# Second products of a two-matmul FFN issued in column halves of 256, and the last row's output evicted in quarters

## The chip, the cores and the metric

The kernel runs on one core of one Trainium2 chip. The metric is the device time of one execution in microseconds; the median of three runs is compared. TensorE multiplies, ScalarE (ACT), VectorE (DVE) and GpSimd (POOL) work elementwise, SyncE (SP) issues the DMAs.

## The reference

Windowed attention followed by a feed-forward network. Four batches, 8 heads, 768 positions, head size 64. Each position attends to its neighbours closer than 16 and to 24 block summaries (the maximum of 32 keys, the mean of 32 values). The heads of a position are joined to a row of 512, and the rows go through the network:

```python
x = attn_out.transpose(0, 2, 1, 3).reshape(B * S, H * D)      # 3072 x 512
h = x @ w_in                                                   # 512 -> 2048
r = np.maximum(h, 0.0)
g = s * (r * r) + b
out = g @ w_out                                                # 2048 -> 512
```

All is float32. The kernel reaches the accuracy by splitting each float32 operand into an upper part of the type fp32r and a lower part of the same type (what the upper leaves over), and adding three products: upper by lower, lower by upper, upper by upper.

## The kernel before

The 3072 rows are cut into 12 chunk rows ("c") of 256 rows. The hidden size 2048 is cut into 16 steps ("f") of 128. For each (c, f) there are:

- `hidden` (L444): the first products. Twelve matmuls of 256 columns into the PSUM tile `ph`: three terms by four slices of the 512 inputs. Stationary are slices of `wl_in` or `wh` (the lower and upper parts of w_in), moving are `xh` or `xl`.
- `activate`, `scaled`, `split_rows`: ScalarE's Relu (L452) and Square (L458), GpSimd's scale and offset (L466), VectorE's split into `gh` (L471) and `gl` (L473).
- `project` (L488): the second products. The 256 rows are two row halves t = 0, 1 of 128; each has a PSUM tile `po[t]` of 128x512, one bank, in which all 16 steps of a chunk row add up. Per t there are three matmuls of 512 columns: stationary is a 128x128 slice of `gl` or `gh`, moving is `w_h["out", f]` or `w_l["out", f]` ("wh" and "wl_out" in the profile; the upper parts of w_in and w_out of a step share a tile called wh).
- `evict` (L498 issues its DMA): after step 15 ScalarE copies `po[t]` to SBUF (the copy's line is L230, a helper; VectorE's copies are L228), and SP sends 256 KB to the output.

In chunk row 0 eight of the steps use plain float32 with one matmul instead of three; the other 184 (c, f) have three terms. The attention of the next chunk row is woven in between: transposes of the probabilities (pt, L358), products with the values (pav, L394), scores (ps, L308).

The order of the work is written out by the program, not found by a scheduler. A table gives the order for the first two chunk rows and the start of the third; after that every piece is put into `plan` at a step number i = 16 c + f with a rank within the step, and each engine's queue has its instructions in the order in which the pieces were called. The hidden products of four steps stand together (`i - i % 4`), and the second products of those four steps come together one group later (`(i + 4) | 3`). So TensorE's queue runs: 48 matmuls of hidden products, perhaps a piece of attention, 24 matmuls of second products, and again. After the last chunk row's hidden products two groups of second products follow each other, 48 matmuls, and then the two evictions.

Of the kernel before, what the change touches and what calls it, by code (L numbers as in the profile page):

```python
# [11 lines left out]
F32 = mybir.dt.float32  # L12
# [7 lines left out]
P = 128  # L20
B, H, S, D = 4, 8, 768, 64
DM, DFF = 512, 2048
# [7 lines left out]
T = NSUB * SUB  # L30
NPAIR = H // 2
PER_B = S // T
NC = B * PER_B
NST = S // SUB
NKC = DM // P
NF = DFF // P
# [8 lines left out]
def windowed_attention_then_relu2_ffn(ctx, tc, qk, vwin, kt, vt, kq, vrow, wp, out):  # L45


    nc = tc.nc
# [4 lines left out]
    stage = ctx.enter_context(tc.tile_pool(name="stage", bufs=4))  # L53
# [37 lines left out]
    def at(step, order, fn, *args):  # L91
        plan[step].append((order, len(plan[step]), fn, args))
# [5 lines left out]
    for base, sign in ((0, 1), (BLOCK - 1, -1)):  # L98
        nc.gpsimd.affine_select(
            out=mean4[:, NB - 4 : NB], in_=mean4[:, NB - 4 : NB], compare_op=ALU.is_ge, fill=0.0,  # L100
# [8 lines left out]
    def steps(c):  # L109
        return SECOND if c == 1 else tuple(range(NF))  # L110
# [32 lines left out]
    def whole(key):  # L143
        uses[key] += 1
        return w_f[key] if uses[key] < (2 if key[1] in THREE else 3) else w_f.pop(key)
# [80 lines left out]
    def copy(by_dve, out_, in_):  # L226
        if by_dve:
            nc.vector.tensor_copy(out_, in_)  # L228
        else:
            nc.scalar.copy(out_, in_)  # L230
# [7 lines left out]
    def place(c):  # L238
        return c // PER_B, c % PER_B
# [182 lines left out]
    ph_of, ph_both, r_of, gg, po = {}, {}, {}, {}, {}  # L422
# [50 lines left out]
        nc.vector.tensor_tensor(gl, g, gh.bitcast(F32), ALU.subtract)  # L473
        gg[c, f] = gh, gl

    def project(c, f):
        if f == steps(c)[0]:
            for t in range(T // P):
                po[t] = ps_po.tile([P, DM], F32, name="po", tag="po")
        g = gg.pop((c, f))  # L480
        if c == 0 and f not in THREE:
            terms = [(g[0], whole(("out", f)))]
        else:
            gh, gl = g
            terms = [(gl, w_h["out", f]), (gh, w_l["out", f]), (gh, w_h["out", f])]
        for t in range(T // P):
            for n, (a, w) in enumerate(terms):
                nc.tensor.matmul(  # L488
                    po[t], a[:, t * P : (t + 1) * P], w,
                    start=(f == steps(c)[0] and n == 0), stop=(f == steps(c)[-1] and n == len(terms) - 1),  # L490
                )

    def evict(c, t, other=False):
        o = stage.tile([P, DM], F32, name="o", tag="stage")
        copy(other, o, po[t])
        bi, ci = place(c)
        r0 = bi * S + ci * T + t * P
        nc.sync.dma_start(out[r0 : r0 + P, :], o)  # L498


    LOAD, SPLIT, ATT, NEXT, WEIGHTS, HID, PE_ATT, CHAIN, VISIT, PROJ, EVICT = range(11)
# [34 lines left out]
    def of(fn, s):  # L536
# [8 lines left out]
        "Ai": of(scale_weights, "in"), "Ao": of(scale_weights, "out"), "Bi": of(convert_weights, "in"),  # L545
        "Bo": of(convert_weights, "out"), "D": lambda f: convert_weights(("in", f), ("out", f)),
        "Y": hidden_part, "H": hidden, "J": activate, "G": scaled, "g": split_rows, "P": project, "O": evict,
        "hi": of(upper_weights, "in"), "ho": of(upper_weights, "out"), "li": of(lower_weights, "in"),
        "lo": of(lower_weights, "out"),
# [18 lines left out]
    def then(step, order, fn, *args):  # L568
        if (fn, args) not in ahead:
            at(step, order, fn, *args)  # L570

    for c in range(2, NC):
        bi, ci = place(c)
        for p in range(NPAIR):
# [3 lines left out]
            m, e0, e1, n, fv, tr, tu, va, xa = (base + lag for lag in lags)  # L578
# [27 lines left out]
    for i in range(NF, NC * NF):  # L606
        c, j = divmod(i, NF)
        f = steps(c)[j]

        then(i - i % 4, HID, hidden, c, f)  # L610
        for stage_of in (activate, scaled, split_rows):
            then(i, CHAIN, stage_of, c, f)
        then((i + 4) | 3, PROJ, project, c, f)
        if j == NF - 1:
            for t in range(T // P):
                then((i + 4) | 3, EVICT, evict, c, t)
# [60 lines left out]
```

## Time and profile before

| what | value |
|---|---|
| median of the runs | 630.85 us (630.57 to 630.95, 3 runs) |
| profiled execution | 630.93 us, its span 629.2 us |
| TensorE matmuls busy | 616.5 us, 5330 matmuls and as many weight loads |
| VectorE, ScalarE, GpSimd busy | 328.3, 308.7, 187.7 us |
| second products with three terms (L488) | 3 x 368 matmuls of 512 columns, mean 392 to 397 ns from start to end |
| hidden products with three terms (L444) | 3 x 704 matmuls of 256 columns, mean 276 to 278 ns |

Matmuls overlap: one starts long before the one ahead of it has ended. The mean duration is therefore not the pace; the pace is the distance between starts, which the chain of waits (length of a block over its number of matmuls) and the timeline show. "PEld" is the weight load that stands before each matmul.

### The profile page before, as it was taken

The page shows a single profiled execution, that of the slowest core. Times are in us where ns is not written, and L with a number is a line of the kernel's source. Part 1 is how long each engine was busy: PE and PEld are TensorE (multiplying, and loading weights), DVE is VectorE, ACT ScalarE, POOL GpSimd, SP SyncE. Part 2 cuts the span into 40 slices and gives each one's busy share as a digit, 9 for nine tenths or more (in the row PEclk, how much of TensorE's full clock was granted, in tenths as well). Part 3 has the DMA queues.
Part 4 walks back from the last instruction along what each step waited for, and adds up shares of the span by engine and source line. Part 5 has one row for each costly group of instructions (what it writes and reads, how often), then busy time and mean ns, then how long its engine had stood idle before and what let it go on. Part 6 is the DMA issues. An engine that isn't in the chain of part 4 may idle for free.

```text
span 629.2 us, 14328 instructions
## 1 busy us (share of the span) xinstructions
PE 616.5 (98%) x5330; PEld 550.7 (88%) x5330; DVE 328.3 (52%) x1092; ACT 308.7 (49%) x939; POOL 187.7 (30%) x351
## 2 busy tenths in 40 slices
PE   6999999999999999999999999999999999999997
PEld 5757878989989998999899999998998999899896
DVE  6999899865354246345454335336435324523311
ACT  4999975453463364265245426436345336323321
POOL 3126442211511422322242331341151151232211
PEclk9999999999999999999999999999999999999999
DMA  8999503006205015203502211600710500200000
GB/s 333 413 416 416 222 26 126 17 2 190 79 18 181 1 44 200 74 19 102 165 20 87 94 44 38 236 19 1 218 62 7 181 0 19 85 2 1 34 1 33
DMA packets 26997, 66.45 MB, mean 106 GB/s; under 512 B 3824, under 2 KB 3824, under 8 KB 26928
## 3 DMA queue, kind: packets, MB, share of 16 engines
q1 hardware_dynamic: 26928, 65.54, 29.3%
q8 instruction: 42, 0.69, 0.5%
q14 instruction: 27, 0.22, 0.1%
HBM read 59.09 MB, written 6.29 MB: 104 GB/s over the span
## 4 chain that ended last, share of the span: by engine, by line
PE 87%; DVE 4%; ACT 2%; issue 1%; POOL 1%; DVEq 0%; POOLq 0%; ACTq 0%
PE po L488 40%; PE ph L444 38%; PE pav L394 3%; PE pt L358 3%; PE ps L308 3%; DVE wf_out L141 1%; POOL g L466 1%; DVE wl_in L155 1%; DVE wf_in L141 0%; DVE wf_in L139 0%; ACT r L458 0%; DVE wf_out L139 0%; ACT wraw L125 0%; ACT wraw L126 0%; ACT r L452 0%
## 5 line engine op out<-in xcount | busy, mean ns | idle before, releaser
L466 POOL TENSOR_SCALAR g<-r,sb_col 128x256 f32<-128x256 f32 x189 | 127.1, 673 | 379.2 <-ACT r L458 256.0
L471 DVE CAST gh<-g 128x256 fp32r<-128x256 f32 x184 | 54.9, 298 | 244.0 <-POOL g L466 244.0
L452 ACT ACTIVATE r<-ph 128x256 f32<-128x256 f32 x179 | 67.6, 378 | 206.1 <-PE ph L444 187.0
L488 PE MATMUL po<-wh,gl 128*128 128x512 f32 x368 | 146.3, 397 | 0.0
L488 PE MATMUL po<-wh,gh 128*128 128x512 f32 x368 | 145.0, 394 | 0.0
L488 PE MATMUL po<-wl_out,gh 128*128 128x512 f32 x368 | 144.2, 392 | 0.0
L444 PE MATMUL ph<-xh,wl_in 128*128 128x256 f32 x704 | 109.9, 278 | 0.1
L444 PE MATMUL ph<-xl,wh 128*128 128x256 f32 x704 | 108.8, 276 | 0.0
L444 PE MATMUL ph<-xh,wh 128*128 128x256 f32 x704 | 108.7, 276 | 0.0
L473 DVE TENSOR_TENSOR gl<-g,gh 128x256 fp32r<-128x256 f32 x184 | 85.8, 466 | 33.6 <-PE po L488 16.4
L444 PEld LDWEIGHTS ph<-xh,wl_in 128*128 128x128 f32 x704 | 96.8, 188 | 4.8 <-issue 0.5
L444 PEld LDWEIGHTS ph<-xl,wh 128*128 128x128 f32 x704 | 93.6, 188 | 0.0
L444 PEld LDWEIGHTS ph<-xh,wh 128*128 128x128 f32 x704 | 93.0, 188 | 0.0
L339 ACT ACTIVATE pr<-pr,mn 128x120 f32<-128x120 f32 x176 | 67.0, 382 | 38.6 <-DVE mn L326 38.4
L458 ACT ACTIVATE r<-r 128x256 f32<-128x256 f32 x184 | 77.0, 418 | 15.2 <-DVE r L454 9.7
L488 PEld LDWEIGHTS po<-wh,gl 128*128 128x128 f32 x368 | 69.1, 188 | 14.8 <-issue 1.4
L488 PEld LDWEIGHTS po<-wh,gh 128*128 128x128 f32 x368 | 69.2, 188 | 14.3
L488 PEld LDWEIGHTS po<-wl_out,gh 128*128 128x128 f32 x368 | 69.2, 188 | 13.8
L270 POOL COPY vw<-vsum 24x256 f32<-24x256 f32 x88 | 41.7, 503 | 20.9 <-DMA vsum<-vmean 9.5
L230 ACT COPY o<-po 128x512 f32<-128x512 f32 x24 | 14.0, 589 | 42.3 <-PE po L488 41.3
L339 ACT ACTIVATION_READ_ACCUMULATOR pr<-pr,mn 128x1 f32 x176 | 33.0, 187 | 0.0
L349 DVE TENSOR_TENSOR pr<-pr,rs 128x480 f32<-128x480 f32 x48 | 32.0, 666 | 1.7
(90 smaller groups left out, 565.4 us busy)
## 6 DMA issues: line engine op xcount, KB each, us to landing
wraw<-in_wp_dram SPq DMA_DIRECT2D x32, 512.0 KB
qk<-in_qk_dram SPq DMA_DIRECT2D x44, 369.0 KB
vw<-in_vwin_dram SPq DMA_DIRECT2D x48, 256.0 KB
out_dram<-o SPq DMA_DIRECT2D x24, 256.0 KB
kraw<-in_kt_dram SPq DMA_DIRECT2D x12, 384.0 KB
vraw<-in_vt_dram SPq DMA_DIRECT2D x12, 252.0 KB
kq<-in_kq_dram SPq DMA_DIRECT2D x4, 512.0 KB
vraw<-in_vt_dram SPq DMA_DIRECT2D x6, 264.0 KB
```

Of the source, the lines that this page charges most:

```text
L270: nc.gpsimd.tensor_copy(vw_t[c, p][WIN:KR, e], vsum[bi][WIN : WIN + NB, 2 * p + e, :].unsqueeze(1).to_broadcast([NB, NSUB, D]),)
L308: nc.tensor.matmul(o, qi, kw[r, i, :], start=True, stop=True)
L339: nc.scalar.activation(pr, pr, AF.Exp, bias=mn_of[c, p][:, n : n + 1], scale=-1.0, accum_out=sm_of[c, p][:, n : n + 1])
L349: nc.vector.tensor_tensor(pr, pr, rs.unsqueeze(2).to_broadcast([P, 4, KR]), ALU.mult)
L358: nc.tensor.transpose(pt_of[c, p][:KR, n * P : (n + 1) * P], pr[:, n, :], ident)
L444: nc.tensor.matmul(ph, w[:, kc * P : (kc + 1) * P], x[:, kc], start=(n == 0), stop=(n == len(terms) - 1))
L452: nc.scalar.activation(r, ph, AF.Relu)
L458: nc.scalar.activation(r, r, AF.Square)
L466: (nc.vector if other else nc.gpsimd).tensor_scalar(g, r_of.pop((c, f)), s_col, b_col, ALU.mult, ALU.add)
L471: nc.vector.tensor_copy(gh, g)
L473: nc.vector.tensor_tensor(gl, g, gh.bitcast(F32), ALU.subtract)
L488: nc.tensor.matmul(po[t], a[:, t * P : (t + 1) * P], w, start=(f == steps(c)[0] and n == 0), stop=(f == steps(c)[-1] and n == len(terms) - 1),
```

## The change

Two parts. First, every three-term second product is issued in two halves of 256 columns: for each row half the three terms go to columns 0 to 255 and then to columns 256 to 511. The one-term products of chunk row 0 stay at 512 columns. Only the first matmul of a bank carries the start flag.

Second, in the last chunk row the last four steps are no longer taken step by step with both row halves each: all four steps are done for row half 0, then for row half 1. A new `evict_last` takes the place of the two evictions there: each 128x512 row half goes out as two tiles of 128x256, the left one copied by ScalarE, the right one by VectorE, with a DMA of 128 KB each.

```diff
-    def project(c, f):
+    def project(c, f, only=None):
...
-        g = gg.pop((c, f))
+        g = gg[c, f] if only == 0 else gg.pop((c, f))
...
-        for t in range(T // P):
-            for n, (a, w) in enumerate(terms):
-                nc.tensor.matmul(
-                    po[t], a[:, t * P : (t + 1) * P], w,
-                    start=(f == steps(c)[0] and n == 0), stop=(f == steps(c)[-1] and n == len(terms) - 1),
-                )
+        size = DM // 2 if len(terms) > 1 else DM
+        for t in range(T // P) if only is None else (only,):
+            for d in range(0, DM, size):
+                for n, (a, w) in enumerate(terms):
+                    nc.tensor.matmul(
+                        po[t][:, d : d + size], a[:, t * P : (t + 1) * P], w[:, d : d + size],
+                        start=(f == steps(c)[0] and n == 0 and d == 0),
+                        stop=(f == steps(c)[-1] and n == len(terms) - 1 and d == DM - size),
+                    )
...
+    def evict_last():
+        half = DM // 2
+        for t in range(T // P):
+            bi, ci = place(NC - 1)
+            r0 = bi * S + ci * T + t * P
+            for d in range(2):
+                o = stage.tile([P, half], F32, name="o", tag="stage")
+                copy(d == 1, o, po[t][:, d * half : (d + 1) * half])
+                nc.sync.dma_start(out[r0 : r0 + P, d * half : (d + 1) * half], o)
...
+        if c == NC - 1 and j >= NF - 4:
+            for t in range(T // P):
+                then((i + 4) | 3, PROJ + t, project, c, f, t)
+            if j == NF - 1:
+                then((i + 4) | 3, EVICT + 1, evict_last)
+            continue
```

TensorE's queue at one step of the second products, before: two row halves, three matmuls each (the number in a name tells tiles apart).

```order
L488 MATMUL po<-wh_745,gl 128x512
L488 MATMUL po<-wl_out_1040,gh 128x512
L488 MATMUL po<-wh_745,gh 128x512
L488 MATMUL po<-wh_745,gl 128x512
L488 MATMUL po<-wl_out_1040,gh 128x512
L488 MATMUL po<-wh_745,gh 128x512
```

The same step after the change:

```order
L490 MATMUL po<-wh_745,gl 128x256
L490 MATMUL po<-wl_out_1040,gh 128x256
L490 MATMUL po<-wh_745,gh 128x256
L490 MATMUL po<-wh_745,gl 128x256
L490 MATMUL po<-wl_out_1040,gh 128x256
L490 MATMUL po<-wh_745,gh 128x256
L490 MATMUL po<-wh_745,gl 128x256
L490 MATMUL po<-wl_out_1040,gh 128x256
L490 MATMUL po<-wh_745,gh 128x256
L490 MATMUL po<-wh_745,gl 128x256
L490 MATMUL po<-wl_out_1040,gh 128x256
L490 MATMUL po<-wh_745,gh 128x256
```

Twelve matmuls of half the width stand where six stood, each with its weight load; nothing moved in or out between them.

The end of ScalarE's queue and of SP's, before:

```order
L452 ACTIVATE r<-ph 128x256
L458 ACTIVATE r<-r 128x256
L230 COPY o<-po 128x512 x2
```

```order
L259 DMA vw<-in_vwin_dram 128x512 x3
L498 DMA out_dram<-o 128x512 x4
```

The ends of ScalarE's, VectorE's and SP's queues after it:

```order
L452 ACTIVATE r<-ph 128x256
L458 ACTIVATE r<-r 128x256
L230 COPY o<-po 128x256 x2
```

```order
L471 CAST gh<-g 128x256
L473 TENSOR_TENSOR gl<-g,gh 128x256
L228 COPY o<-po 128x256 x2
```

```order
L259 DMA vw<-in_vwin_dram 128x512 x3
L501 DMA out_dram<-o 128x512 x2
L511 DMA out_dram<-o 128x256 x4
```

ScalarE's two copies are halved, VectorE has two more at its end, and SP's last two DMAs became four of half the size. VectorE's copy of a bank waits for ScalarE's copy of the same bank in the compiled program.

## The prediction

> **What bounds the kernel now.** I read the page first, then the busy time by stretches, then the chain in order of time, and last single matmuls in the timeline. From the page, the span, TensorE's two rows (matmuls and weight loads) and the chain:
>
> ```profile
> span 629.2 us, 14328 instructions
> PE 616.5 (98%) x5330; PEld 550.7 (88%) x5330; DVE 328.3 (52%) x1092; ACT 308.7 (49%) x939; POOL 187.7 (30%) x351
> PEclk9999999999999999999999999999999999999999
> ...
> PE po L488 40%; PE ph L444 38%; PE pav L394 3%; PE pt L358 3%; PE ps L308 3%; DVE wf_out L141 1%; POOL g L466 1%; DVE wl_in L155 1%; DVE wf_in L141 0%; DVE wf_in L139 0%; ACT r L458 0%; DVE wf_out L139 0%; ACT wraw L125 0%; ACT wraw L126 0%; ACT r L452 0%
> ```
>
> The second products (po, L488) and the first ones (ph, L444) hold 78% of the chain. By stretches (length, then busy time of PE, PEld, DVE, ACT, POOL):
>
> ```profile
> 60.00:112.00 52.00, 50.24 (x381) 44.07 (x374) 47.73 (x132) 37.71 (x99) 19.19 (x27) 1.00 0.38 136
> 112.00:160.00 48.00, 48.00 (x423) 43.79 (x422) 34.17 (x105) 21.95 (x70) 11.93 (x19) 1.00 0.30 90
> 160.00:400.00 240.00, 240.00 (x2100) 218.82 (x2099) 106.56 (x399) 109.59 (x359) 72.38 (x138) 1.00 0.25 82
> 400.00:600.00 200.00, 200.00 (x1685) 182.45 (x1684) 81.21 (x279) 81.82 (x256) 57.06 (x108) 1.00 0.17 56
> ```
>
> From 112 us on TensorE never waits, at full clock, and no other engine is near its limit. What counts is the pace of its matmuls. The chain gives it by blocks, here the first TensorE block on it, one chunk row, and the end:
>
> ```profile
> 81.88 3.11 PE ph L444 x24
> ...
> 224.91 5.70 PE po L488 x24
> 230.61 5.47 PE ph L444 x48
> 236.08 5.49 PE po L488 x24
> 241.57 5.47 PE ph L444 x48
> 247.04 0.87 PE pt L358 x8
> 247.91 5.51 PE po L488 x24
> 253.43 5.46 PE ph L444 x48
> 258.89 0.87 PE pt L358 x8
> ```
>
> A block of 24 matmuls of 512 columns takes as long as one of 48 of 256. Both load a new 128x128 weight for every matmul, so the hidden stage is already the shape that the change gives the second products. The timeline resolves the pace (start, duration; a row of x4 is four matmuls):
>
> ```profile
> 609.00 0.64 PE L444 MATMUL ph<-xh,wl_in 128*128 128x256 f32 x4
> ...
> 610.39 0.62 PE L444 MATMUL ph<-xh,wl_in 128*128 128x256 f32 x4
> ...
> 614.47 0.39 PE L488 MATMUL po<-wh,gl 128*128 128x512 f32 x1
> ...
> 625.23 0.40 PE L488 MATMUL po<-wh,gh 128*128 128x512 f32 x1
> ```
>
> From 614.47 to 625.23 lie 47 steps of 512 columns: 10.76 / 47 = 228.9 ns each. From 610.39 to 614.47 lie 36 steps of 256: 4.08 / 36 = 113.3 ns. The first 12 of that block took 1.39 us, 115.8 ns each: a block that follows 512-column matmuls needs some steps to reach its pace, and that costs 1.39 - 12 x 0.1133 = 0.03 us.
>
> **The change, part by part.**
>
> 1. *Halves.* 1104 three-term matmuls (three groups of 368) become 2208 of 256 columns with 2208 weight loads. 24 of the 1104 lie before 81.88 us, where the chain is on other engines; 1080 count. Two halves at the settled pace are 226.7 ns against 228.9, a gain of 2.2 to 2.3 ns each: -2.4 us. I take the settled pace of the hidden stage because the instruction pair has the same form: an fp32r weight load of 128 columns, then 256 columns streamed. The other end is below under the rivals.
>
> 2. *Block starts.* 39 blocks of hidden products that now follow 512-column products will follow 256-column ones and need no settling: -39 x 0.03 = -1.2 us. 30 blocks of second products that start after transposes (pt) or after the value and score products (pav, ps) may have to settle themselves: +30 x 0.03 = +0.9 us. The 88 to 110 ns that such a block loses now (5.70 or 5.51 against 5.49 us) is its first weight load, which nothing covers; it stays. Net -0.3 us, between -1.2 and +0.9.
>
> 3. *More instructions.* 2208 more on TensorE's queue. The hidden stage issues at the same rate now without a gap, so this is put at nothing; cover gone, it would show as the settling cost above on every pair.
>
> 4. *Last four steps by row half.* The same 48 matmuls (96 halves) in another order. Step 12's operands come first in both orders; the last step's gl is needed about 9 x 0.23 = 2 us after the first of these products instead of 18 x 0.23 = 4 us. VectorE's last gl ends here, against products that start at 614.47 + 24 x 0.229 = 620.0 us, so nothing waits:
>
> ```profile
> 617.62 0.43 DVE L473 TENSOR_TENSOR gl<-g,gh 128x256 fp32r<-128x256 f32 x1
> ```
>
> 5. *The end.* Now:
>
> ```profile
> 624.97 1.28 ACT L230 COPY o<-po 128x512 f32<-128x512 f32 x2 [8.69 <-PE po L488]
> ...
> 625.58 1.02 SPq L498 DMA_DIRECT2D out_dram<-o  x2
> ```
>
> and the nearest copies of 256 columns out of PSUM:
>
> ```profile
> L452 ACT ACTIVATE r<-ph 128x256 f32<-128x256 f32 x179 | 67.6, 378 | 206.1 <-PE ph L444 187.0
> L230 ACT COPY o<-po 128x512 f32<-128x512 f32 x24 | 14.0, 589 | 42.3 <-PE po L488 41.3
> L228 DVE COPY xh<-pav 128x256 f32<-128x256 f32 x2 | 0.8, 418 | 0.0
> ```
>
> The first row half and its two DMAs go out some 24 x 0.113 = 2.7 us earlier, under the second half's products. Behind the last matmul stand one copy of 589 ns and a 256 KB transfer now. Then there are ScalarE's quarter, 378 ns, and VectorE's, 418 ns, which in the compiled order waits for ScalarE's, so the two copies of one bank go in turn: 796 ns and a handoff of some 50, about 0.26 us later. In return the last transfer is half as large and no longer queues behind the other row half. Two transfers of 256 KB end within the stretch from 625.23 to 629.20, which moved 132 GB/s x 3.97 us = 0.52 MB:
>
> ```profile
> 625.23:629.20 3.97, 0.39 (x2) 0.00 (x0) 0.00 (x0) 0.91 (x2) 0.00 (x0) 1.00 0.34 132
> ```
>
> Its 16 engines were busy 0.34 x 3.97 = 1.35 us for both, so half of one is 0.34 us. -0.34 + 0.26 = -0.1; I put the end at 0, from -0.4 (the two copies side by side) to +0.3 (the smaller transfer lands no sooner). SP issues two DMAs more; behind them in its queue is nothing but the end.
>
> *Sum.* -2.4 - 0.3 + 0 = -2.7 us. The profiled execution took 630.93 us (span 629.2 and 1.7 around it), the median of the runs is 630.85. 630.93 - 2.7 - 0.08 = 628.2 us.
>
> **A rule that speaks against it.** By the rows, a halved matmul has no fixed cost: 2 x 113.3 is below 228.9. The Trainium skill (TensorE: Matmul & The Clock Gate, Back-to-back issue gap) gives a warm matmul N / 2.4 GHz plus about 2.5 ns whatever its size. By that each split costs 2.5 ns, an estimate of 1080 x 2.5 = +2.7 us and 633.6 us in all. The rows differ from the page in both shapes (228.9 against 215.8, 113.3 against 109.2 ns), and I follow them.
>
> **The rivals.**
>
> *A. The halves don't settle (slower).* The settled pace leaves no room: weight load and matmul both take about 113 ns, while under 512 columns the load has 229 ns. And the trace has hidden blocks that never settle:
>
> ```profile
> 130.89 0.63 PE L444 MATMUL ph<-xh,wl_in 128*128 128x256 f32 x4
> ...
> 136.54 0.40 PE L488 MATMUL po<-wh,gl 128*128 128x512 f32 x1
> ```
>
> 48 steps in 5.65 us are 117.7 ns each, to the last one. What decides is how the block starts. Two blocks that start after transposes, as second products do, show both (steps 5 to 8 of each):
>
> ```profile
> 118.61 0.64 PE L444 MATMUL ph<-xl,wh 128*128 128x256 f32 x4
> 119.08 0.64 PE L444 MATMUL ph<-xh,wh 128*128 128x256 f32 x4
> ...
> 120.47 0.62 PE L444 MATMUL ph<-xl,wh 128*128 128x256 f32 x4
> 120.92 0.28 PE L444 MATMUL ph<-xh,wh 128*128 128x256 f32 x1
> ```
>
> 0.47 us for four in the first (117.5 ns), 0.45 in the second (113). For it speaks that in the changed kernel every run of halves starts after pt, or after pav and ps, with an uncovered weight load. Against it: hidden blocks after 160 us all settle (5.46 or 5.47 us). Price: an unsettled block of products 48 x 0.1177 = 5.65 against 24 x 0.2289 = 5.49 now, +0.16; the hidden block that runs on from it 5.65 against 5.47, +0.18. All 45 blocks of products (1080 / 24) and 39 hidden ones: +7.2 + 7.0 = +14.2 us, 645. There are three kinds of start in a chunk row: after pav and ps (half of the matmuls run on from it) and after the two pt pairs (a quarter each). A quarter unsettled: 0.75 x -2.7 + 0.25 x 14.2 = +1.5, 632.4; half: +5.8, 636.6. It decides from a share of 2.7 / 16.9 = 16% on.
>
> *B. A cost per matmul (slower).* If switching weights in every half keeps the second products at the pace of the first 12 steps of a block, 115.8 ns, a pair costs 231.6, +2.7 ns each: 1080 x 2.7 = +2.9, less the 0.3: 633.4 us. For it: weights alternate with every matmul and the PSUM bank with every six. Against it: the hidden stage changes its weights as often and settles. The rule of the Trainium skill cited above (TensorE: Matmul & The Clock Gate, Back-to-back issue gap) would come out near this time.
>
> *C. It moves the time by nothing that can be told.* If the halves run at the mean of a hidden block with its start, 5.47 / 48 = 114.0, a pair takes 228.0 against 228.9: -1.0 us, and with the end at +0.2, 630.0. Blocks 5.49 and 5.47 us long speak for it; that the settled pace lasts longer over joined blocks, against it.
>
> **How the numbers follow.** Settled, 628.2: 0.48, with its own range 627.0 to 629.4 (items 1, 2 and 5 at their ends). C: 0.12. A with a quarter unsettled 0.13, with half 0.13, with more 0.08; B 0.06. A difference of 0.2%, 1.26 us, is about what a measurement of this kernel can tell. Faster 0.48, same 0.12, slower 0.13 + 0.13 + 0.08 + 0.06 = 0.40. The range reaches from 627.0 to A's half at 637.0; outside remain the rest of A and a little below, about 0.12.
>
> **What the changed profile would show.** If right: po blocks of 48 at 5.44 to 5.47 us on the chain, hidden blocks at 5.44, starts of settled stretches 113.3 ns apart; the last copy some 0.9 us after the last matmul and its DMA shorter. If A: blocks of 5.65 us in both stages, the same ones in each chunk row. If B: po blocks of 5.55 with hidden blocks unchanged. What would make it wrong is A: a phase between weight loads and matmuls that the trace shows but that I can't compute for the new starts.

## The result, and the profile after

| | before | after |
|---|---|---|
| median of the runs | 630.75 us (4 runs) | 637.99 us (637.78 to 638.96, 4 runs) |
| profiled execution, span | 630.93, 629.2 us | 638.04, 636.3 us |
| ratio, 95% interval | | 1.0118, 1.01 to 1.0135 |

The change makes the kernel 1.2% slower: +7.2 us by the medians, +7.1 by the profiled executions, where -2.7 was forecast. It is rival A. From the page after, the span, TensorE's rows and the chain by line:

```profile
span 636.3 us, 16544 instructions
...
PE 624.5 (98%) x6434; PEld 605.3 (95%) x6434; DVE 329.8 (52%) x1094; ACT 308.3 (48%) x939; POOL 183.9 (29%) x351
...
PEclk9999999999999999999999999999999999999999
...
PE po L490 40%; PE ph L444 38%; PE pav L394 3%; PE ps L308 3%; PE pt L358 3%; DMA wraw<-in_wp_dram 1%; POOL g L466 1%; DVE wf_out L141 1%; DVE wf_in L141 1%; DVE wf_in L139 1%; ACT pr L339 1%; DVE wl_in L155 1%; DVE pr L326 0%; DVE pr L349 0%; ACT r L458 0%
```

The shares are those of before; TensorE is busy 8.0 us longer. By stretches (length, then PE, PEld, DVE, ACT, POOL busy, granted clock):

```profile
112.00:160.00 48.00, 48.00 (x511) 47.65 (x510) 33.90 (x105) 21.94 (x70) 11.31 (x19) 1.00 0.29 86
160.00:400.00 240.00, 240.00 (x2541) 238.22 (x2540) 105.44 (x395) 107.32 (x354) 70.98 (x136) 1.00 0.24 78
400.00:600.00 200.00, 200.00 (x2051) 198.74 (x2049) 81.11 (x279) 82.83 (x259) 56.55 (x108) 1.00 0.19 63
```

As before, TensorE never waits from 112 us on, at full clock. So no other engine took the time; its own pace did. The chain in order of time, two chunk rows' pieces:

```profile
226.11 5.85 PE po L490 x48
231.96 5.66 PE ph L444 x48
237.62 5.65 PE po L490 x48
243.27 5.46 PE ph L444 x48
248.72 0.87 PE pt L358 x8
249.60 5.45 PE po L490 x48
255.05 5.66 PE ph L444 x48
...
276.50 5.85 PE po L490 x48
282.36 5.45 PE ph L444 x48
287.81 5.44 PE po L490 x48
293.25 5.66 PE ph L444 x48
```

Before, all such blocks took 5.46 to 5.51 us from 160 us on (5.70 behind scores). Now each block of either stage has one of two lengths, 5.45 or 5.65 us (5.85 for a slow one behind scores), and the two mix without regard to the stage. The timeline shows the pace inside a block. Two products 13 steps apart in the block that starts at 237.45 us, and two in the block at 287.65:

```profile
237.57 0.28 PE L490 MATMUL po<-wl_out,gh 128*128 128x256 f32 x1
...
239.10 0.28 PE L490 MATMUL po<-wh,gh 128*128 128x256 f32 x1
```

```profile
287.65 0.28 PE L490 MATMUL po<-wh,gl 128*128 128x256 f32 x1
...
289.12 0.28 PE L490 MATMUL po<-wl_out,gh 128*128 128x256 f32 x1
```

13 steps in 1.53 us are 117.7 ns each; 13 steps in 1.47 us, 113.1. These are the two paces that the prediction read from hidden blocks. Below, a block is called slow when it runs at the longer one and settled when it runs at the shorter one. In this trace a settled block has its pace after its first few products, some of which are 117 to 124 ns apart, and a slow one keeps 117.7 ns to its end.

The end, from the start of the last matmul, then the two last copies:

```profile
632.44:636.32 3.88, 0.28 (x3) 0.09 (x1) 0.42 (x1) 0.37 (x1) 0.00 (x0) 1.00 0.20 70
```

```profile
632.76 0.37 ACT L230 COPY o<-po 128x256 f32<-128x256 f32 x1 [2.35 <-PE po L490]
```

```profile
633.16 0.42 DVE L228 COPY o<-po 128x256 f32<-128x256 f32 x1 [2.30 <-ACT o L230]
```

3.88 us stand behind the last matmul's start, 3.97 before.

The two stages account for the loss. I summed the distances from block start to block start from 112 us on, and counted a block as slow where the 256-column products of its second half came more than 115 ns apart (41 hidden and 42 product blocks are long enough for that; the other rows are the experiments below):

| kernel | slow product blocks | slow hidden blocks | product blocks, us | hidden blocks, us |
|---|---|---|---|---|
| before | (512 wide) | 1 of 41 | 237.6 | 224.1 |
| after | 31 of 42 | 19 of 41 | 241.6 | 227.3 |
| halves_only | 31 | 19 | 241.6 | 227.3 |
| terms_outer | 31 | 19 | 241.6 | 227.3 |
| last_whole | 29 | 10 | 241.0 | 225.6 |
| shorter_4 | 34 | 25 | 242.5 | 228.5 |
| shorter_8 | 34 | 24 | 242.3 | 228.3 |
| shorter_16 | 42 | 13 | 243.7 | 226.0 |
| first_whole | 26 | 20 | 240.6 | 227.5 |
| ends_whole | 13 | 2 | 237.9 | 224.1 |
| settled_only | 1, 21 left whole | 1 | 236.9 | 224.1 |
| first_six | 7 | 0 | 236.9 | 223.8 |
| mostly_halves | 0, 7 left whole | 0 | 236.2 | 223.9 |

After against before: 4.0 in the product blocks, 3.1 in the hidden ones that nobody edited, -0.1 at the end: 7.0 of 7.1. The attention pieces (pt, pav, ps) are the same to 0.01 us each. The same blocks are slow in after, halves_only and terms_outer, one for one, so the order is not chance.

### The profile page after: what moved, and what is told of

Read it like the earlier page. It is cut to its first block, busy times and chain, and to the rows that moved or that the text cites. A ratio compares the mean times of both kernels' runs of the same rounds, so it can differ in the third digit from the quotient of the medians.

```text
span 636.3 us, 16544 instructions
## 1 busy us (share of the span) xinstructions
PE 624.5 (98%) x6434; PEld 605.3 (95%) x6434; DVE 329.8 (52%) x1094; ACT 308.3 (48%) x939; POOL 183.9 (29%) x351
## 4 chain that ended last, share of the span: by engine, by line
PE 87%; DVE 6%; ACT 2%; issue 2%; DMA 1%; POOL 1%; SPq 0%; DVEq 0%; POOLq 0%
PE po L490 40%; PE ph L444 38%; PE pav L394 3%; PE ps L308 3%; PE pt L358 3%; DMA wraw<-in_wp_dram 1%; POOL g L466 1%; DVE wf_out L141 1%; DVE wf_in L141 1%; DVE wf_in L139 1%; ACT pr L339 1%; DVE wl_in L155 1%; DVE pr L326 0%; DVE pr L349 0%; ACT r L458 0%
## 5 line engine op out<-in xcount | busy, mean ns | idle before, releaser
L490 PE MATMUL po<-wh,gl 128*128 128x256 f32 x736 | 208.1, 283 | 0.0
L490 PE MATMUL po<-wh,gh 128*128 128x256 f32 x736 | 205.1, 279 | 0.0
L490 PE MATMUL po<-wl_out,gh 128*128 128x256 f32 x736 | 205.1, 279 | 0.0
L490 PEld LDWEIGHTS po<-wh,gl 128*128 128x128 f32 x736 | 138.3, 188 | 1.7 <-issue 1.3
L490 PEld LDWEIGHTS po<-wl_out,gh 128*128 128x128 f32 x736 | 138.3, 188 | 0.0
L490 PEld LDWEIGHTS po<-wh,gh 128*128 128x128 f32 x736 | 138.3, 188 | 0.0
L444 PE MATMUL ph<-xh,wh 128*128 128x256 f32 x704 | 110.1, 279 | 0.0
L444 PEld LDWEIGHTS ph<-xh,wl_in 128*128 128x128 f32 x704 | 94.6, 189 | 0.4 <-issue 0.3
L270 POOL COPY vw<-vsum 24x256 f32<-24x256 f32 x88 | 39.7, 481 | 22.9 <-PE po L490 10.9
L230 ACT COPY o<-po 128x512 f32<-128x512 f32 (+1 forms) x24 | 13.6, 569 | 42.8 <-PE po L490 41.7
```

The costliest lines, as they stand in the source:

```text
L270: nc.gpsimd.tensor_copy(vw_t[c, p][WIN:KR, e], vsum[bi][WIN : WIN + NB, 2 * p + e, :].unsqueeze(1).to_broadcast([NB, NSUB, D]),)
L444: nc.tensor.matmul(ph, w[:, kc * P : (kc + 1) * P], x[:, kc], start=(n == 0), stop=(n == len(terms) - 1))
L490: nc.tensor.matmul(po[t][:, d : d + size], a[:, t * P : (t + 1) * P], w[:, d : d + size], start=(f == steps(c)[0] and n == 0 and d == 0), ...
```

## The experiments

Theory P: each block of 256-column products runs at 113.3 or 117.7 ns, and which one is decided as it begins. Rival Q: every switch between the column halves of a bank, or every halved product, has a cost of its own. Rival R: a block is slow because of what it waits for, or what runs beside it.

**Which part of the change.** `tail_only` has the last row's part alone and stays 512 wide.

```diff
-        size = DM // 2 if len(terms) > 1 else DM
+        size = DM
```

> The second part of the change alone: all second products 512 columns wide as before, the last four steps by row half and the output in quarters. Theory P (two paces: a run of 256-column matmuls that each load their weights has no slack and goes at 113.3 or at 117.8 ns a matmul, set where a block begins; 512-column matmuls have slack and keep 228.9): 630.6 us, 0.1 below before, product blocks of 24 at 5.49 to 5.61 us and hidden blocks of 48 at 5.46 to 5.56 as before. Rival Q (each switch between the column halves of a bank costs a little, wherever it stands): the same here. If the tail carried part of the loss it would show as a time above 631.5.

630.58 us against 630.57 for before on the same chip, ratio 1.0002 (0.9992 to 1.0011). Its end on the chain:

```profile
614.52 11.00 PE po L490 x48
...
625.55 0.38 ACT o L230
...
625.95 0.42 DVE o L228
```

The two quarters do go in turn. Whatever the smaller last transfer wins, the sum of the second part is nothing that can be told. `halves_only` is the first part alone; the lines that order the last four steps and call `evict_last` are out.

```diff
-        if c == NC - 1 and j >= NF - 4:
-            ...
-            continue
```

> The first part alone: halves of 256 columns, the last steps and the evictions as before. Both theories: the whole loss, 638.1 us (0.1 above the change). P also expects the same blocks at 117.8 as in the changed kernel up to the last chunk row, since nothing ahead of them differs; Q expects every product block slower by the same amount.

638.06 us, ratio 1.0118 (1.0103 to 1.0133), block sums as in after: the whole loss.

**The switch between halves.** `terms_outer` changes the half at every product.

```diff
-            for d in range(0, DM, size):
-                for n, (a, w) in enumerate(terms):
+            for n, (a, w) in enumerate(terms):
+                for d in range(0, DM, size):
```

> As the changed kernel, but each term does its two column halves in turn (the same stationary columns loaded twice in a row), so that the half changes at every product instead of every third. Rival Q (each switch between the halves costs, or the load of a new weight): three times as many switches, three times the loss by switches, about 652; if a repeated weight is free, under 631. Theory P: the switch costs nothing, the blocks are at 113.3 or 117.7 in some order again: 631 to 645 with the two paces and none between.

638.5 us in one run, of which 1.0 us is a longer end (4.90 us behind the last matmul's start, 3.88 in after). With three times as many switches, the same blocks are slow, one for one, as in halves_only, and the block sums equal after's to 0.01 us (241.61 and 227.26). A switch costs nothing, and loading the same stationary columns twice in a row saves nothing. Q's first form is out.

**What a block begins with.** `last_whole` leaves the last three products of each group of 48 at 512 columns.

```diff
+        place_in_four = steps(c).index(f) % 4
...
+            last = place_in_four == 3 and t == T // P - 1
+            size = DM if len(terms) == 1 or last else DM // 2
```

> As the change, but in each group of four steps the last row half of the fourth step keeps its three matmuls 512 columns wide, so that every hidden block follows 512-column matmuls as it did before. P: the 17 slow hidden blocks (5.65 us) are gone, all at 5.46 to 5.47: 3.1 us less; product blocks stay mixed between 113.3 and 117.8; about 634.9 us, within 2 us since product blocks that follow a hidden block directly may fall either way. Q: the slow hidden blocks have nothing to do with the products' width and stay; the products lose an eighth of their 4.0 us: about 637.5.

635.68 us, ratio 1.0077 (1.0061 to 1.0094). P's 634.9 lies in the interval (634.4 to 636.5 on this chip's 630.57), Q's 637.5 above it. The chain:

```profile
275.79 5.84 PE po L492 x45
281.63 5.47 PE ph L444 x48
287.10 5.45 PE po L492 x45
...
298.89 5.65 PE po L492 x45
```

Three wide products at the end of a group, and slow hidden blocks fall from 19 to 10, though nothing in the hidden blocks differs. P had expected none; the ten that stay slow all stand behind a slow product block, so three wide products do not settle what follows every time. The product blocks keep a mix (29 slow). `first_whole` has the wide products at the head of the group instead (`last = place_in_four == 0 and t == 0`).

> Against the changed kernel: only the first three products of each group of 48 stay 512 wide. Theory P: the end of the group is as in the changed kernel (a half at 113.3 or 117.7), so the hidden blocks stay mixed (about 227 us in all), and the product blocks have another order of fast and slow than in the changed kernel: 632 to 639, with the product blocks settled if a whole product ahead settles them (632.5), mixed else (636.5). Rival Q: 42 of 48 halves, 637.

638.38 us in one run (span 636.7), above P's 636.5 for the mixed case, 1.0 us of it again a longer end (4.87 us): 20 hidden blocks slow, 26 product blocks. A wide head alone settles neither stage. `ends_whole` has both (`(place_in_four, t) in ((0, 0), (3, T // P - 1))`).

> Against the changed kernel: the first three and the last three products of each group of 48 stay 512 wide, the 36 halves between them remain. last_whole (last three whole) left 35 of 42 hidden blocks settled (225.61 us of hidden blocks, 224.12 before), but about 27 of 42 product blocks slow. Theory P (the state of a block is set by how it begins): with whole products at both ends the hidden blocks are as before, 224.1 us; if the halves behind settled whole products settle as well, each block has 6 x 228.9 + 36 x 113.3 ns = 5.45 us and the time is 630.8 - 42 x 36 x 1.1 ns = 629.0; if the product blocks keep their mix of paces (27 of 42 at 117.7), 42 x 36 x 0.64 x 4.4 ns = 4.3 us more, 633.3. Rival Q (each switch between the column halves costs): 36 of 48 halves keep three quarters of the loss, 636.

631.00 us, ratio 1.0003 (0.9993 to 1.0013), between P's two cases and far from Q's 636. The hidden blocks are back at 224.1 us.

```profile
274.81 5.66 PE po L492 x42
280.46 5.47 PE ph L444 x48
285.93 5.45 PE po L492 x42
...
297.73 5.46 PE po L492 x42
...
309.54 5.63 PE po L492 x42
```

29 of 42 product blocks are settled. From the third chunk row on, those behind a hidden block or behind scores always are (5.45, 5.66); of those behind transposes one of two per chunk row is slow (5.63 against 5.46), and one behind the values of the last-but-one row.

**Is it the moment of the start?** `shorter_4`, `shorter_8` and `shorter_16` are halves_only with the second product of each group cut by 4, 8 or 16 columns.

```diff
+                    n_cols = size - 4 if len(terms) > 1 and place_in_four == 0 and t == d == 0 and n == 1 else size
...
-                        po[t][:, d : d + size], a[:, t * P : (t + 1) * P], w[:, d : d + size],
+                        po[t][:, d : d + n_cols], a[:, t * P : (t + 1) * P], w[:, d : d + n_cols],
```

> The second product of each group of four steps streams 252 columns instead of 256 (4 columns of one partial sum per group are left out), all else as in halves_only (638.06 us, 16 of about 42 hidden blocks and 29 of 42 product blocks at 117.7 ns, in the same order every two chunk rows). The columns alone are worth 42 x 4 / 2.4 GHz = 0.07 us. Theory P (the pace of a block, 113.3 or 117.7 ns, is set by the phase at which its products begin against a grid of 6.67 ns, 8 cycles of 1.2 GHz or 16 columns): a shift of a quarter of the grid near the start of each block changes which blocks are slow, in the product blocks and in the hidden blocks behind them, so the order of fast and slow blocks differs from that of halves_only; the time moves by up to 3 us either way, to 631-645. Rival R (a block is slow because of what it waits for or what runs beside it on DVE, ACT or the queues): the same blocks are slow, 638.0 within 0.4 us.

> As shorter_4 with 8 columns less (248), half of the 6.67 ns grid. Theory P: another order of fast and slow blocks than in halves_only and in shorter_4, the time anywhere from 631 to 645. Rival R: the same blocks slow as in halves_only, 637.9 within 0.4 us.

> As shorter_4 with 16 columns less (240), which is one whole period of the 6.67 ns grid. Theory P: the phase behind the shorter product is the one of halves_only, so the same blocks are slow, and the time is that of halves_only less 42 x 16 / 2.4 GHz = 0.28 us: 637.8 within 0.4 us. Rival R: the same, 637.8; this run tells P from R only together with shorter_4 and shorter_8. A theory by which any shorter product unsettles or settles a block alike expects the order of shorter_4 and shorter_8 here too.

640.05, 640.13 and 638.6 us in one run each; before on that chip 630.9. Leaving out 0.07 us of work makes the kernel 2 us slower than halves_only (2.1 us by the block sums). In the chain of shorter_4 the product block behind scores (5.85 in after) is settled and its neighbours, settled in after, are slow:

```profile
276.57 5.65 PE po L492 x48
282.23 5.66 PE ph L444 x48
287.88 5.65 PE po L492 x48
293.54 5.66 PE ph L444 x48
```

The shift is 1.7 ns: in slow product blocks from 170 us on the third product starts 117.5 ns behind the second in halves_only and 115.8 ns in shorter_4 (means). The engines' queues are the same, but their work falls a little differently beside later blocks, so R needs a closer look. Some hidden blocks have nothing beside them as they begin. Two of halves_only, then one of shorter_4 (length, then PE, PEld, DVE, ACT, POOL busy, granted clock, DMA share and GB/s):

```profile
216.15:217.90 1.75, 1.75 (x17) 1.75 (x16) 0.00 (x0) 0.00 (x0) 0.00 (x0) 1.00 0.00 0
266.74:268.49 1.75, 1.75 (x18) 1.75 (x17) 0.00 (x0) 0.00 (x0) 0.00 (x0) 1.00 0.00 0
```

```profile
216.74:218.49 1.75, 1.75 (x18) 1.75 (x17) 0.00 (x0) 0.00 (x0) 0.00 (x0) 1.00 0.00 0
```

No other engine and no DMA is busy there, and TensorE does not wait, yet the first block is slow (5.65 us on the chain) and the other two are settled (5.46 and 5.45). So R is out as the cause. But the finer part of P fell too. shorter_8 should have had another order than shorter_4, and has the same one from the third chunk row on; shorter_16 should have brought back the order of halves_only, and brought a third one (42 product blocks and 13 hidden ones slow). So, as far as these runs show, the timing around a block's start decides, and the grid of 6.67 ns that I had set down for it isn't shown.

**What the two paces are made of.** `narrow_weights` halves the stationary columns in all steps but the first and last of a chunk row; it leaves out half of the rows of those products.

```diff
+        rows = P if len(terms) == 1 or f in (steps(c)[0], steps(c)[-1]) else P // 2
...
+                        po[t][:rows, d : d + size], a[:, t * P : t * P + rows], w[:, d : d + size],
```

> As the change, but in steps 2 to 15 of each chunk row the halves load only 64 of the 128 stationary columns and compute only the upper 64 rows of each row half (the first and the last step are whole); columns streamed and matmuls stay as many. P: the weight load is then far shorter than the matmul, so there is slack again: no product block at 117.8 except perhaps next to the whole steps, pace 113.3 or a little less, product blocks 5.44 to 5.55, hidden blocks mostly settled: 628.4 to 631.5 us. Q: the number of switches is the same, so about 637 us with blocks at 5.65.

637.64 us in one run: a miss. The loads did become shorter (rows of the groups by line, mean in ns):

```profile
L444 PEld LDWEIGHTS ph<-xh,wl_in 128*128 128x128 f32 x704 | 94.7, 189 | 0.5 <-issue 0.4
...
L491 PEld LDWEIGHTS po<-wh,gl 128*64 128x64 f32 x644 | 86.2, 134 | 1.7 <-issue 1.4 <-DVE xl L410 0.2
```

but the blocks did not:

```profile
261.62 5.60 PE po L491 x48
```

5.60 / 48 = 116.7 ns, and 36 of 42 product blocks are slow. With loads of half the columns the slow pace is 1 ns shorter and does not go away, so the weight load's length does not make it. `fewer_columns` keeps the 128-column loads and streams 192 columns in those steps.

```diff
+        cols = size if len(terms) == 1 or f in (steps(c)[0], steps(c)[-1]) else 192
...
+                        po[t][:, d : d + cols], a[:, t * P : (t + 1) * P], w[:, d : d + cols],
```

> The product halves of the second to the fifteenth step of each chunk row stream 192 columns instead of 256 (1932 products of 2208; a quarter of the columns of their partial sums is left out). narrow_weights halved the stationary columns and kept both paces (113.3 and 116.7), so theory P in its new form has it that the stream with a gap, and not the weight load, sets the pace: 192 / 2.4 GHz = 80 ns and a gap of 6.7 to 11 ns, 87 to 91 ns a product, 1932 x 26 ns = 50 us less: 585 to 592 us. If a fixed cost of a load and a product in turn sets it (the old form), the pace stays at 107 ns or more and the time at 625 us or more.

628.84 us in one run: a quarter of the columns gone, and 9 us gained where P in its new form had 50. That form fell, and the old one, a pace of 107 ns or more, held.

```profile
307.98 5.34 PE po L491 x48
```

5.34 / 48 = 111.3 ns. `narrow_fewer` has 64 stationary and 192 streamed columns.

> narrow_weights and fewer_columns together: in the second to the fifteenth step of each chunk row the product halves have 64 stationary columns and stream 192 (three quarters of the sums left out or cut). 64 stationary columns and 256 streamed had 113.3 and 116.7 ns a product, 128 and 192 had 111.5. If there are two limits, a load of 128 columns every 111 ns and a stream of its columns with a gap of 6.7 to 11 ns, both are gone here: 87 to 91 ns a product, 1932 x 26 ns less than in narrow_weights, 586 to 592 us. If a load and a product in turn cost a fixed 111 ns whatever their widths, the time stays at 626 to 629.

589.61 us in one run, as the two limits had it.

```profile
294.94 4.23 PE po L492 x48
```

4.23 / 48 = 88.1 ns. So there are two limits, 1.8% apart: a new weight of 128 columns every 111.3 ns, and 256 streamed columns every 113.3 at best. The Trainium skill (TensorE: Matmul & The Clock Gate, LDWEIGHTS) has a load take its stationary columns / 1.2 GHz, 106.7 ns for 128 and 53.3 for 64. The trace agrees in the difference (189 - 134 = 55 ns less for 64 columns less) and nearly in the floor of 111.3; from start to end the loads show 189 and 134 ns.

**Are the paces all of it?** If so, halves must pay where they settle. `settled_only` is ends_whole with halves only in 22 groups, all but one of which were settled there.

```diff
+            last = (place_in_four, t) in ((0, 0), (3, T // P - 1)) or c < 2 or (c < NC - 1 and group < 2)
```

> As ends_whole, but halves only in the groups that were settled there: the third and fourth group of each chunk row from the third row on (they come behind scores or a hidden block) and all four of the last row, 22 of 44 groups; the groups behind transposes and those of the first two rows stay 512 wide throughout. Theory P (the two paces are the whole loss): a settled group in ends_whole took 5.454 us behind a hidden block and 5.566 behind scores, against 5.494 and 5.606 before, 0.040 us less, which is 36 x (114.45 - 113.33) ns; 22 x 0.040 = 0.9 us less than before, 629.9 us, ratio 0.9986, with the hidden blocks at 224.1 as before. Rival Q (a halved product costs something of its own beside the paces): at or above the time before, 630.8 or more. If a phase carried over from the whole groups unsettles the halves, 22 x 36 x 4.4 ns = 3.5 us at most more, 634.

630.03 us against 630.57, ratio 0.999 (0.9981 to 0.9999). The gain of a settled block is the one expected:

```profile
274.43 5.66 PE po L492 x42
280.09 5.47 PE ph L444 x48
285.55 5.45 PE po L492 x42
...
297.35 5.50 PE po L492 x24
```

5.45 in halves where before has 5.49. `first_six` has six wide products at the head of the groups behind transposes.

```diff
+            last = ... or (place_in_four == 0 and c < NC - 1 and group < 2)
```

> As ends_whole, but in the groups behind transposes (first two of each chunk row but the last) the first six products are whole instead of three, 30 halves between. In ends_whole 10 of 20 such groups were slow (5.72 us against 5.54). Theory P with a product that settles within the whole ones: if six whole products ahead bring the group behind transposes to the same phase each time and it settles, 10 x 0.17 us less than ends_whole, 629.2 us; if three more products only shift the phase, some are slow as before, 631. The block's pace stays one of two (113.3, 117.7) in either case.

630.41 us against 630.57, ratio 0.9995 (0.9986 to 1.0004): of the 18 groups behind transposes that the trace has from the third chunk row on, 5 are slow, where ends_whole had 9 (not 10, as the expectation has it). The outcome lies between P's two cases. `mostly_halves` leaves the groups that were slow there wholly at 512 columns.

```diff
+            last = last or (group == 0 and c % 2 == 0 and c < NC - 1) or (c, group) in ((1, 2), (NC - 2, 2))
```

> As first_six, but the groups that were slow there (the first group of every second chunk row from the third on, one group of the second row and the one behind the values of the last but one) are 512 wide throughout. Theory P: the product blocks fall from 236.9 us by 5 x (5.702 - 5.596) + (5.756 - 5.626) + 0.10 = 0.76 us to 236.1, the hidden blocks stay at 223.8; against before (237.6 and 224.1) 1.8 us less, 629.0 us, ratio 0.9972. If the whole groups bring the next ones behind transposes to another phase, up to ten of them are slow, 30 x 4.4 ns = 0.13 us each, 630.3. Rival Q (a cost of the halves beside the paces) has the time at or above that of settled_only, 630.0.

629.80 us against 630.80, ratio 0.998 (0.997 to 0.999), the lowest of the versions that compute the whole result, and no slow block in either stage:

```profile
273.55 5.66 PE po L493 x42
279.20 5.47 PE ph L444 x48
284.67 5.45 PE po L493 x42
...
296.47 5.47 PE po L493 x39
```

The block sums came out within 0.1 us of those expected (236.2 and 223.9 us), 1.6 us under before's. The median is 1.0 under, and the expected ratio 0.9972 lies in the interval; in the profiled execution the end took 5.05 us instead of 3.97, where one part of the last transfer landed 0.45 us behind the rest. Q's second form, a cost of the halved product itself, is out: 657 of the 1104 three-term products are halved here, and the kernel is faster than with none.

## Why the prediction was wrong

*Item 1, halves, is the step that failed.* Its size was right where its condition held: 18 halved pairs in a settled block save 0.040 us, 2.2 ns a pair. The condition was the settled pace, and I took it because the instruction pair has the same form, and set A aside because "hidden blocks after 160 us all settle". All of those stood behind 512-column products, and that is what the change took away. In after 31 of 42 product blocks and 19 of 41 hidden ones ran at 117.7 ns; with three wide products at the end of each group 10 hidden blocks were slow, with three at both ends 2. The trace of before had no row of a 256-column block behind another in the steady part, so it could not carry 0.48. The blocks settled under a condition that the edit removed. Nor was that condition safe: the slow hidden block that the prediction shows stood behind 512-column products, and the 512-column block behind it was slow too, which the prediction passed over:

```profile
131.05 5.66 PE ph L444 x48
136.70 5.60 PE po L488 x24
```

Its products came 233.3 ns apart, 228.6 in the others. So P's clause in tail_only's expectation, that wide products have slack and keep 228.9 ns, doesn't hold either; in this trace one of 42 blocks of them was slow.

*Item 2, block starts.* A settled hidden block behind halves took 5.45 us instead of 5.466, so about 0.01 and not 0.03 was to be had, in 22 blocks; 18 more than before were slow and lost 0.19 each. The sign of the net was wrong.

*Item 3, more instructions.* That 256 columns issue without a gap held; its clause "cover gone, it would show as the settling cost above on every pair" came true in 50 of 83 blocks, block by block and at a higher price (6.5 ns a pair, see B).

*Items 4 and 5* held: tail_only is 630.58 against 630.57, and the end is 3.88 us in after and 4.15 in tail_only against 3.97, where 0 (-0.4 to +0.3) was put.

*Rival A* had the mechanism and the prices. 31 + 19 slow of 83 are 60%; by its own formula 0.40 x -2.7 + 0.60 x 14.2 = +7.4, measured +7.1. Its trace sign was "the same ones in each chunk row"; the order repeats every two. Its chance of 0.34 in all was too low, and "half" or "more" deserved most of it. Its reason, that load and matmul both take about 113 ns, is half shown: both limits are there (111.3 and 113.3), but with the load halved the slow pace stayed (116.7).

*Rival B and the rule beside it.* The rule of the Trainium skill (TensorE: Matmul & The Clock Gate, Back-to-back issue gap) would have cost 2.5 ns per split; the section gives it for isolated matmuls. The trace disagrees: settled halves gain 2.2 ns a pair, and slow ones lose 2 x 117.7 - 228.9 = 6.5. That its 633.6 lies nearer the result is chance.

*Open.* What inside TensorE holds a block at 117.7 ns, and which start leads to which pace, is not shown. That 1.7 ns among the first products of each group changes which blocks are slow, also blocks that begin with nothing else busy beside them, is.

## What to carry to other kernels

A pace read from a block holds under the conditions in which that block begins; before you carry it over, list what precedes it, and ask whether the edit removes that. Where two limits lie within 2% of each other (here weight load and stream), splitting work down to that point buys little; here it also put code next to it on a slower pace, for a reason that stays open, so look at the neighbours that were not edited. If such a split is kept, try wide products where stages meet: in this kernel three at each end of a group took the loss away, and the best mix found was worth 0.2%.

## What the runs showed of the hardware that was not expected

- Two paces for products of 256 fp32r columns with a new 128-column weight each, 113.3 and 117.7 ns, kept from a block's first few products to its end (the first block behind 112 us changed its pace midway in four of the other runs). Which one an unedited stage takes changed with the width of the products ahead of it (of 41 hidden blocks 1 was slow in before, 19 in after, 10 in last_whole, 2 in ends_whole). Four streamed columns fewer per group (1.7 ns) changed which blocks had which, and cost 2 us.
- Products of 512 columns have a second pace too: one block behind a slow one came at 233.3 ns instead of 228.6.
- 192 columns with a new 128-column weight came 111.3 ns apart, hardly faster than 256; with 64 stationary columns, 88.1.
- A quarter of the streamed columns of 1932 products left out was worth 9.2 us (637.99 to 628.84, one run) and not 50.
